# A new written order of all steps, and PSUM as four buffers whose halves serve single-bank steps

## The chip, the cores and the metric

The kernel runs on one core of a Trainium2 chip. The metric is the device time of one execution in microseconds (us). Five engines take part, each with its own instruction queue that is worked off in order: PE (TensorE, matrix products and transposes; the profile shows its weight loads apart, as PEld), ACT (ScalarE), DVE (VectorE), POOL (GpSimd) and SP (SyncE), which here only issues DMA transfers. An engine waits at an instruction until everything that the instruction needs is there, and what stands behind it in the same queue waits too.

## What is computed

Blockwise causal attention over 8 batches, 8 heads, 576 positions and 64 dimensions, followed by a gated unit with a causal convolution in its gate. Cut to what matters:

```python
scores = q @ k.transpose(0, 1, 3, 2) / sqrt(64)
scores = where(block_i >= block_j, scores, -1e9)      # blocks of 64 positions
attn = softmax(scores)
x = (attn @ v).transpose(0, 2, 1, 3).reshape(8, 576, 512)
gate_pre = sum(conv_w[k] * xp[:, k:k + 576, :] for k in range(5))   # xp: x with 4 zero rows ahead
gate = 1 / (1 + exp(-gate_pre))
out = (gate * (x @ w_val)) @ w_out
```

## The kernel before

The work is cut into steps. A step is a Python function under `@op` that issues a few instructions of one kind on one engine; the text `PLAN` lists all 961 steps in the order in which they are issued. A word such as `S/1.0/P/2` means: step `S`, for pair 1, part 0, on PE, into PSUM buffer 2. `V`, `A`, `G`, `S`, `P` stand for DVE, ACT, POOL, SP and PE. Each engine's queue is the list's words for that engine, in the list's order, so nothing is planned at run time: the list is the plan. The framework adds the waits between engines that the data and the buffers ask for.

Attention works on 32 pairs of heads (four pairs to a batch). For a pair `p`:

- `lq`, `lk`, `lv` load its q, k and v (256 KB, 256 KB and two of 128 KB). `lt` and `lvt` load the last 64 positions of all heads of a batch. All are issued by SP, but for one `lk` of ACT.
- `cq`, `cv`, `ct`, `cvt` cast what was loaded to fp16, mostly on POOL (`cq0` is pair 0's `cq` in two halves).
- `T` transposes q and k on PE (8 transposes of 128 columns) into one PSUM bank; `Te` copies the result to SBUF. `T0`, `T0e` are the same for pair 0 in halves; `TT`, `TTe` for the tails of a batch.
- `S/p.t` (t = 0, 1, 2) forms scores with 64 contraction rows, both heads side by side in two banks; `E/p.t` takes their exponential on ACT (128 x 1024 elements). `SL`, `EL` are the last key block of all heads of a batch. `mka`, `mkb` write zeros over the masked corners, on POOL.
- `A` (30 products of 65 columns) multiplies by v, with a column of ones that yields the sums; `N` divides on DVE; `X` transposes the result back on PE (5 transposes) and `Xe` copies it to the gated unit's input.

The gated unit works on 16 half batches `n`: `C` (80 products on 32 x 32 pieces of the array) is the convolution into two 2-bank buffers, `CS` the gate's tanh on ACT, `V` the value projection (8 products of 288 columns, two steps per `n`), `Ve` the product of both on DVE. `O` is the output projection of 128 rows (4 products of 512 columns), `Oe` copies it to SBUF, `Od` stores it; the last 128 rows go in two halves as `OL`, `OLe`, `OLd`. Once at the start, `CW` brings the convolution's weights onto partitions with a fp32 product, and `CWe` builds from them the pieces that `C` uses; `lwv`, `cwv` load and cast the value weights; `lwo`, `cwo`, `W`, `We` load, cast and reorder the output weights. `w0` is a filler: products of zeros that nothing reads. `pact` is an exponential of one element, ahead of which the activation table is loaded.

The loads and casts have few buffers: five for q and k, five for v, four for transposed q and k, four for exponentials, six for output rows, two for tails. SP's queue holds loads and stores together, so a store that waits for its copy holds the loads behind it.

PSUM has eight banks. Before, `PP` (line 142) makes three buffers of two banks, 0 to 2, and two of one bank, 3 and 4. A step that needs two banks (`S`, `SL`, `A`, `V`, half a `C`) takes a buffer of 0 to 2; a step that needs one bank (`T`, `X`, `TT`, `W`, `O`, `OL`) takes buffer 3 or 4, or the first bank of one of the others. `one(b)` (line 145) gives the bank of a single-bank step.

Single lines carry many steps: line 127 is every product, line 322 the transposes of `T`, 354 those of `TT`, 453 those of `X`, lines 192 and 194 every copy on ACT and on DVE or POOL, 388 `E`, 410 and 412 `mka`, 416 `mkb`, 444 and 445 `N`.

Of the kernel before, what the change touches and what calls it, by code (L numbers as in the profile page):

```python
# [12 lines left out]
lk/1/S pact//A ppool//G lq/1/S lk/0/A lq/0/S lt/0.1/S pdve//V cq0/1/A w0/14/P/4 cq/1/G lt/0.0/S  # L13
lk/2/S lcv//S lq/2/S T/1/P/2 cq/2/G Te/1/A lq/3/S cq0/0/V lk/3/S S/1.0/P/2 lvt/0/S T0/1/P/3 E/1.0/A
T0e/1/V S/1.1/P/1 T0/0/P/0 lk/4/S T0e/0/A E/1.1/A lt/1.0/S lt/1.1/S S/0.1/P/0 cq/3/V lq/4/S ct/0/G
E/0.1/A S/0.0/P/1 TT/0/P/2 lv/0.0/S TTe/0/V E/0.0/A T/2/P/3 lv/0.1/S lq/5/S S/0.2/P/0 SL/0/P/2
Te/2/V S/1.2/P/1 T/3/P/4 Te/3/V lk/5/S lv/1.1/S CW//P/3 lv/1.0/S cvt/0/G cv/0/V E/0.2/A lk/6/S
lq/6/S E/1.2/A S/2.1/P/0 lv/3.1/S mka/0/G S/2.2/P/1 lvt/1/S ct/1/G TT/1/P/4 lv/2.0/S lv/3.0/S EL/0/A
mkb/1/G E/2.1/A S/3.0/P/2 CWe//V cq/4/G mkb/0/G A/0/P/0 TTe/1/V E/2.2/A N/0/V S/3.1/P/1 T/4/P/4
cq/5/G S/2.0/P/0 mka/1/G cv/1/G E/3.0/A E/3.1/A T/5/P/3 mkb/2/G lv/2.1/S cq/6/G S/3.2/P/1 E/2.0/A  # L20
Te/4/V lv/4.1/S mka/3/G E/3.2/A Te/5/V A/1/P/2 SL/1/P/0 S/4.1/P/1 EL/1/A T/6/P/3 N/1/V mka/2/G
cv/2/V lk/7/S S/4.0/P/0 X/0/P/4 cvt/1/G lwo/1/S mkb/3/G cv/3/G lv/4.0/S Te/6/V E/4.1/A S/4.2/P/2
E/4.0/A mka/4/G A/2/P/1 A/3/P/0 lwo/0/S E/4.2/A S/5.1/P/2 cwo/1/G N/2/V X/2/P/3 lq/7/S S/5.0/P/1
lv/5.0/S cv/4/G lv/5.1/S mkb/4/G Xe/0/A lwv/0/S lwv/1/S N/3/V E/5.1/A cq/7/G Xe/2/V lv/6.0/S
S/5.2/P/0 lv/6.1/S cv/5/G E/5.0/A X/3/P/4 Xe/3/V E/5.2/A X/1/P/3 lq/8/S A/4/P/2 lk/8/S Xe/1/V lk/9/S
N/4/V mkb/5/G C/0/P/1+0 CS/0.1/A T/7/P/3 S/6.0/P/2 X/4/P/4 lq/9/S CS/0.0/A lt/2.0/S S/6.2/P/0
cwo/0/G Te/7/V lt/2.1/S Xe/4/V E/6.0/A cwv/1/V lv/7.1/S S/6.1/P/1 E/6.2/A mka/5/G lv/7.0/S W/1/P/3
cwv/0/G E/6.1/A mka/6/G A/5/P/2 mkb/6/G We/1/A V/0.0/P/0 cv/6/G N/5/V cq/8/G cq/9/G S/7.1/P/1
W/3/P/3 W/2/P/4 Ve/0.0/V E/7.1/A lvt/2/S S/7.2/P/0 A/6/P/2 lk/11/S E/7.2/A S/7.0/P/1 ct/2/G W/0/P/0
lv/8.1/S We/2/V cv/7/G We/3/V lq/11/S E/7.0/A T/8/P/3 X/5/P/4 mka/7/G N/6/V Te/8/A lt/3.1/S lv/8.0/S  # L30
lk/10/S C/1/P/1+2 We/0/V S/8.1/P/0 Xe/5/V mkb/7/G TT/2/P/4 CS/1.0/A cq/11/G X/6/P/3 lq/10/S CS/1.1/A
V/0.1/P/1 E/8.1/A TTe/2/V lt/3.0/S Ve/0.1/V S/8.0/P/2 lv/12.0/S T/9/P/4 Xe/6/V E/8.0/A A/7/P/0
mka/8/G S/8.2/P/2 lk/12/S SL/2/P/1 O/0.0/P/3 Te/9/V O/0.1/P/4 EL/2/A E/8.2/A lq/13/S N/7/V cvt/2/G
lv/10.0/S S/9.1/P/0 S/9.2/P/1 mkb/8/G Oe/0.1/V Oe/0.0/A X/7/P/3 E/9.1/A Xe/7/V lv/11.1/S V/1.0/P/2
lv/9.1/S cv/8/G lv/9.0/S E/9.2/A Ve/1.0/V A/8/P/0 ct/3/G S/9.0/P/1 E/9.0/A T/11/P/3 lv/10.1/S
cq/10/G lt/4.1/S Te/11/A mkb/9/G T/10/P/4 lt/4.0/S N/8/V C/2/P/0+2 Te/10/V V/1.1/P/1 CS/2.0/A
lq/12/S S/10.0/P/0 Ve/1.1/V lt/5.1/S CS/2.1/A cv/9/G lq/16/S S/10.1/P/2 E/10.0/A lk/13/S E/10.1/A
TT/3/P/4 mka/9/G TTe/3/V lk/14/S S/10.2/P/1 mka/10/G cv/10/G O/0.3/P/3 E/10.2/A mkb/10/G lv/11.0/S
A/9/P/0 S/11.0/P/2 Oe/0.3/V lk/16/S N/9/V E/11.0/A S/11.1/P/1 lv/14.0/S cq/12/G O/0.2/P/4 A/10/P/0
lq/14/S lk/17/S Oe/0.2/V lv/13.0/S cq/13/G S/11.2/P/2 lq/15/S cv/11/G lv/12.1/S N/10/V T/12/P/3  # L40
lvt/4/S X/8/P/4 E/11.1/A C/3/P/1+0 E/11.2/A mkb/11/G cq/14/G Xe/8/A mka/11/G SL/3/P/2 CS/3.0/A
lvt/3/S Te/12/V EL/3/A CS/3.1/A X/10/P/4 Od/0.1/S lt/5.0/S T/13/P/3 V/2.1/P/1 lv/13.1/S S/12.1/P/2
Xe/10/V Te/13/V V/2.0/P/0 Ve/2.1/V V/3.0/P/1 X/9/P/4 lk/15/S Ve/2.0/V Ve/3.0/V E/12.1/A lv/15.0/S
lv/16.1/S A/11/P/0 S/12.0/P/2 lk/18/S N/11/V S/12.2/P/1 E/12.0/A cv/12/G Od/0.0/S E/12.2/A ct/4/G
O/0.5/P/3 cvt/3/G V/3.1/P/0 Xe/9/V TT/4/P/4 lk/19/S Oe/0.5/V T/14/P/3 S/13.0/P/2 Ve/3.1/V mkb/12/G
TTe/4/A E/13.0/A S/13.1/P/1 lv/15.1/S X/11/P/0 Od/0.2/S Te/14/V mka/12/G lv/16.0/S E/13.1/A
O/0.4/P/4 A/12/P/2 cq/15/G Oe/0.4/A Xe/11/V N/12/V cv/13/G S/13.2/P/0 S/14.0/P/1 mka/13/G O/0.6/P/3
T/15/P/4 E/14.0/A C/4/P/1+2 Oe/0.6/V E/13.2/A mkb/13/G X/12/P/3 cq/16/G CS/4.1/A A/13/P/0 SL/4/P/2
# [12 lines left out]
Te/20/V E/18.0/A lk/25/S Od/0.6/S ct/6/G SL/5/P/0 EL/5/A S/19.0/P/1 cvt/5/G V/6.0/P/2 S/19.2/P/0
mka/18/G mkb/18/G E/19.0/A Ve/6.0/V X/17/P/4 E/19.2/A lq/25/S S/19.1/P/1 Xe/16/V A/18/P/2 cv/20/G
E/19.1/A T/21/P/3 N/18/V lv/22.1/S cv/19/G Te/21/A C/7/P/0+1 CS/7.1/A lq/27/S V/6.1/P/2 lt/7.1/S
T/22/P/3 mkb/19/G S/20.1/P/1 CS/7.0/A Xe/17/V S/20.0/P/0 Ve/6.1/V E/20.1/A E/20.0/A S/20.2/P/2
Te/22/V E/20.2/A O/1.3/P/4 Od/0.5/S V/7.0/P/1 O/1.2/P/3 mka/19/G mka/20/G Oe/1.3/A lk/24/S lq/26/S
S/21.0/P/0 lv/25.0/S cq/25/G cv/21/G E/21.0/A lv/24.0/S Ve/7.0/V Oe/1.2/V lv/24.1/S S/21.2/P/1
lq/24/S TT/6/P/4 mkb/20/G TTe/6/V E/21.2/A cq/23/G lt/7.0/S A/19/P/2 cq/24/G X/18/P/4 A/20/P/0
N/19/V lv/23.1/S N/20/V Xe/18/A lq/28/S lk/28/S Od/1.0/S S/21.1/P/1 S/22.1/P/2 E/21.1/A cv/22/G
lv/25.1/S Od/0.8/S X/19/P/3 O/1.4/P/4 E/22.1/A Xe/19/V Oe/1.4/V mka/21/G C/8/P/1+0 V/7.1/P/2 lq/30/S
CS/8.1/A Ve/7.1/V lv/27.0/S CS/8.0/A X/20/P/3 T/24/P/0 Te/24/V S/22.0/P/1 Xe/20/A SL/6/P/2 T/23/P/4  # L70
lv/27.1/S lk/26/S cv/24/G mkb/21/G O/1.5/P/3 lv/26.0/S cq/28/G S/22.2/P/0 Te/23/V E/22.0/A EL/6/A
A/21/P/1 E/22.2/A S/23.0/P/2 E/23.0/A V/8.0/P/0 T/25/P/4 lv/23.0/S Od/1.4/S N/21/V Ve/8.0/V Oe/1.5/V
# [32 lines left out]
def kernel(  # L105
# [11 lines left out]
    fp32 = mybir.dt.float32  # L117
# [27 lines left out]
    def one(b):  # L145
        return PP[b][0:128, 0]

# [461 lines left out]
```

## Time and profile before

| | |
|---|---|
| median of 3 runs | 201.42 us (200.97 to 202.28) |
| span of the profiled execution | 199.3 us |
| mean granted TensorE clock | 0.957 |
| read from and written to HBM | 30.42 MB and 9.44 MB |

The span runs from the first to the last instruction of one execution. The costliest groups of the profile, with busy time, mean length of one, and idle time ahead of them with its main releaser:

| group | count | busy us | mean ns | idle before us |
|---|---|---|---|---|
| ACT, exponential of scores (L388) | 96 | 93.7 | 1025 | 24.0, PE |
| PE, value projection (L127) | 256 | 37.3 | 291 | 0.0 |
| PE, output projection (L127) | 148 | 36.0 | 374 | 0.0 |
| PE, attention times v (L127) | 896 | 34.5 | 196 | 1.9, POOL |
| POOL, cast of q and k (L194) | 30 | 31.0 | 1043 | 15.4, DMA of q |
| DVE, copy of transposed q and k (L194) | 23 | 27.3 | 1196 | 4.1, PE |
| DVE, division (L445) | 32 | 26.4 | 824 | 1.1 |
| DVE, gate times value (L512) | 32 | 24.1 | 752 | 18.9, PE |
| PE, transposes of q and k (L322) | 256 | 20.8 | 228 | 2.6, POOL |
| DVE, copy of output rows (L194) | 28 | 19.1 | 688 | 10.4, PE |

A busy time of PE counts overlapping products whose ends are modelled; the distance from one product's start to the next says more. The slices of the profile cut the span into 40 equal parts of 5 us. The clock row gives what share of full speed PE was granted.

### The profile page before, as it was taken

What the parts mean: (1) busy time and instruction counts of PE and PEld (TensorE: products, weight loads), DVE (VectorE), ACT (ScalarE), POOL (GpSimd) and SP (SyncE); (2) the same over time, 40 slices, a digit from 0 to 9 for tenths busy, and PEclk for the clock granted to TensorE, in tenths of its full rate; (3) what the DMA queues carried; (4) which work ended last, traced back from release to release, by engine and by line L of the source; (5) the groups of instructions that cost most, each with busy time, mean ns of one, the idle gap of its engine ahead of it and who ended that gap; (6) DMA issues with size and microseconds to landing.
All of it is one profiled execution on the core that took longest, in us unless ns stands there. A gap on an engine that the chain in (4) does not pass through costs nothing.

```text
span 199.3 us, 8575 instructions
## 1 busy us (share of the span) xinstructions
PE 184.3 (92%) x3706; PEld 129.3 (65%) x3706; DVE 121.3 (61%) x193; ACT 139.4 (70%) x172; POOL 85.3 (43%) x201
## 2 busy tenths in 40 slices
PE   6389999699999799999999999999996999999992
PEld 3248677457676677767777776767764766676651
DVE  5047687675676676764666666777655383664562
ACT  3476896749779638798799888679694888643221
POOL 7255656763635535366394084282606041210000
PEclk9855899879999999999999999999999999999999
DMA  5999999999989999999969819991277610421445
GB/s 183 213 230 274 212 272 342 300 187 243 231 171 271 259 217 315 257 236 290 255 159 278 211 38 303 250 293 62 96 199 227 122 56 3 161 104 68 155 154 215
DMA packets 70336, 40.42 MB, mean 203 GB/s; under 512 B 48149, under 2 KB 64789, under 8 KB 70298
## 3 DMA queue, kind: packets, MB, share of 16 engines
q1 hardware_dynamic: 69882, 39.48, 77.6%
q8 instruction: 29, 0.48, 1.1%
q10 hardware_dynamic: 416, 0.39, 0.6%
q14 instruction: 9, 0.07, 0.1%
HBM read 30.42 MB, written 9.44 MB: 200 GB/s over the span
## 4 chain that ended last, share of the span: by engine, by line
PE 75%; DMA 9%; ACT 4%; POOL 4%; issue 3%; DVE 2%; SPq 1%; POOLq 0%; DVEq 0%; ACTq 0%
PE P L127 64%; PE P L322 7%; PE P L453 4%; DMA vs<-in_v_dram 3%; ACT pt L388 3%; DMA vts<-in_v_dram 3%; DMA qks<-in_q_dram 2%; PE P L354 1%; POOL qk L194 1%; DVE x L445 1%; ACT qkT L192 1%; POOL v16t L194 1%; POOL v L194 1%; POOL w_out L194 1%; POOL pt L410 0%
## 5 line engine op out<-in xcount | busy, mean ns | idle before, releaser
L388 ACT ACTIVATE pt<-P 128x1024 f16<-128x1024 f32 x96 | 93.7, 1025 | 24.0 <-PE P L127 22.9
L194 POOL CAST qk<-qks 128x1024 f16<-128x1024 f32 x30 | 31.0, 1043 | 15.4 <-DMA qks<-in_q_dram 10.9
L127 PE MATMUL P<-xt,w_val 128*128 128x288 f16 x256 | 37.3, 291 | 0.0
L127 PEld LDWEIGHTS <-pt 128*128 128x128 f16 x960 | 32.8, 99 | 5.9 <-issue 1.6
L127 PE MATMUL P<-v,pt 128*128 128x65 f16 x896 | 34.5, 196 | 1.9 <-POOL pt L410 0.9
L127 PE MATMUL P<-w_out,gv 128*128 128x512 f16 (+1 forms) x148 | 36.0, 374 | 0.0
L512 DVE SCALAR_TENSOR_TENSOR gv<-th,P 128x576 f16<-128x576 f32 x32 | 24.1, 752 | 18.9 <-PE P L127 15.0
L127 PE MATMUL P<-qkT 64*128 64x256 f16 (+3 forms) x256 | 31.8, 316 | 2.8 <-ACT qkT L192 1.8
L194 DVE COPY qkT<-P 128x1024 f16<-128x1024 f16 (+1 forms) x23 | 27.3, 1196 | 4.1 <-PE P L322 3.9
L127 PEld LDWEIGHTS <-w_val 128*128 128x128 f16 x256 | 23.8, 99 | 8.2 <-issue 1.1
L494 ACT ACTIVATE th<-P 128x576 f32<-128x576 f32 x32 | 19.2, 648 | 12.8 <-PE P L127 12.8
L127 PEld LDWEIGHTS <-qkT 64*128 64x128 f16 x512 | 17.0, 97 | 16.8 <-issue 10.0
L445 DVE TENSOR_TENSOR x<-P,rc 128x640 f16<-128x640 f32 x32 | 26.4, 824 | 1.1
L194 DVE COPY osb<-P 128x512 f32<-128x512 f32 x28 | 19.1, 688 | 10.4 <-PE P L127 8.3
L410 POOL MEMSET pt<- 64x256 f16 x32 | 9.8, 306 | 31.8 <-ACT pt L388 31.1
L322 PE MATMUL P<-ident,qk 128*128 128x128 f16 x256 | 20.8, 228 | 2.6 <-POOL qk L194 2.6
L444 DVE RECIPROCAL rc<-P 128x10 f32<-128x10 f32 x32 | 7.0, 220 | 25.0 <-PE P L127 23.7
L194 POOL CAST v<-vs 128x512 f16<-128x512 f32 x30 | 18.4, 619 | 8.3 <-DMA vs<-in_v_dram 5.0
L322 PEld LDWEIGHTS <-qk 128*128 128x128 f16 x256 | 16.1, 102 | 7.1 <-POOL qk L194 3.4
L127 PEld LDWEIGHTS <-gv 128*128 128x128 f16 x148 | 12.6, 98 | 12.2 <-issue 1.3
L127 PE MATMUL P<-xt,DG 32*32 32x288 f16 x1280 | 16.9, 288 | 0.0
L416 POOL MEMSET pt<- 64x128 f16 x32 | 6.5, 204 | 22.8 <-ACT pt L388 22.1
(57 smaller groups left out, 154.4 us busy)
## 6 DMA issues: line engine op xcount, KB each, us to landing
out_dram<-osb SPq DMA_DIRECT2D x35, 256.0 KB, 3.1
qks<-in_q_dram SPq DMA_DIRECT2D x32, 256.0 KB, 5.3
vs<-in_v_dram SPq DMA_DIRECT2D x64, 128.0 KB, 5.1
qks<-in_k_dram SPq DMA_DIRECT2D x31, 256.0 KB, 5.1
tls<-in_k_dram SPq DMA_DIRECT2D x8, 128.0 KB, 5.9
tls<-in_q_dram SPq DMA_DIRECT2D x8, 128.0 KB, 6.1
vts<-in_v_dram SPq DMA_DIRECT2D x8, 128.0 KB, 5.5
w_out_st<-in_moe_w_out_dram SPq DMA_DIRECT2D x2, 512.0 KB, 6.4
```

The source lines that it names most:

```text
L127: nc.tensor.matmul(out=out, lhsT=lhsT, rhs=rhs, start=start, stop=stop, skip_group_check=True)
L192: nc.scalar.copy(out=out, in_=in_)
L194: (nc.vector if eng == "V" else nc.gpsimd).tensor_copy(out=out, in_=in_)
L322: nc.tensor.transpose(out=r[:, o:o + 128], in_=t[0:128, c, 2 * i:2 * i + 2, 0:64], identity=ident16[0:128, 0:128])
L388: nc.scalar.activation(out=rot(pts, p)[0:128, 0:2, 512 * t:512 * t + 512], in_=PP[where.pop(("S", p, t))][0:128], func=AF.Exp, bias=0.0, s ...
L410: nc.gpsimd.memset(pt[64:128, 0:2, 0:1024].rearrange("p h (t s) -> p h t s", t=2)[:, :, :, 0:64], 0.0)
L416: nc.gpsimd.memset(rot(pts, p)[64:128, 0:2, 1024:1088], 0.0)
L444: nc.vector.reciprocal(out=rc[0:128], in_=r[:, :, :, 64:65])
L445: nc.vector.tensor_tensor(out=rot(x16, p)[0:128].rearrange("p i h d -> p h i d"), in0=r[:, :, :, 0:64], in1=rc[0:128].to_broadcast([128, 2 ...
L453: nc.tensor.transpose(out=half16(bank)[:, 128 * i:128 * i + 128], in_=rot(x16, p)[0:128, i, 0:2, 0:64], identity=ident16[0:128, 0:128])
L494: nc.scalar.activation(out=rot(ths, n)[0:128, 2 * i:2 * i + 2, 0:288], in_=PP[where["C", n][i]][0:128, 0:2, 0:288], func=AF.Tanh, bias=0.0 ...
L512: nc.vector.scalar_tensor_tensor(out=rot(gvs, b // 2)[0:128, 2 * y:2 * y + 2, b % 2, hf, 0:288], in0=rot(ths, n)[0:128, 2 * y:2 * y + 2, 0 ...
```

## The change

Three things change. The list `PLAN` is written anew: the same steps with the same work (each attention and gated-unit step occurs as often as before), in another order, some on another engine, and with other PSUM buffers. Seven filler words take the place of one. The copies of output rows (`Oe`) are 19 on ACT and 16 on DVE instead of 7 and 28; DVE casts q and k of pairs 1, 4 and 5 instead of pair 3, and does both `cwo`; POOL does both `cwv`; three of four `We` are on ACT. The first lines put `lcv` and `CW`, the convolution's weights, ahead of the loads and transposes of q and k, and `pact` behind the first transposes' copies.

PSUM becomes four buffers of two banks. Two-bank steps name a buffer 0 to 3; single-bank steps name a bank 0 to 7, which is half of a buffer. The filler `w0` takes its number of contraction rows as a second argument.

The diff, cut to what the text speaks of:

```diff
@@ PLAN
-lk/1/S pact//A ppool//G lq/1/S lk/0/A lq/0/S lt/0.1/S pdve//V cq0/1/A w0/14/P/4 cq/1/G lt/0.0/S
-lk/2/S lcv//S lq/2/S T/1/P/2 cq/2/G Te/1/A lq/3/S cq0/0/V lk/3/S S/1.0/P/2 lvt/0/S T0/1/P/3 E/1.0/A
-T0e/1/V S/1.1/P/1 T0/0/P/0 lk/4/S T0e/0/A E/1.1/A lt/1.0/S lt/1.1/S S/0.1/P/0 cq/3/V lq/4/S ct/0/G
-E/0.1/A S/0.0/P/1 TT/0/P/2 lv/0.0/S TTe/0/V E/0.0/A T/2/P/3 lv/0.1/S lq/5/S S/0.2/P/0 SL/0/P/2
-Te/2/V S/1.2/P/1 T/3/P/4 Te/3/V lk/5/S lv/1.1/S CW//P/3 lv/1.0/S cvt/0/G cv/0/V E/0.2/A lk/6/S
...
-cwo/0/G Te/7/V lt/2.1/S Xe/4/V E/6.0/A cwv/1/V lv/7.1/S S/6.1/P/1 E/6.2/A mka/5/G lv/7.0/S W/1/P/3
-cwv/0/G E/6.1/A mka/6/G A/5/P/2 mkb/6/G We/1/A V/0.0/P/0 cv/6/G N/5/V cq/8/G cq/9/G S/7.1/P/1
-W/3/P/3 W/2/P/4 Ve/0.0/V E/7.1/A lvt/2/S S/7.2/P/0 A/6/P/2 lk/11/S E/7.2/A S/7.0/P/1 ct/2/G W/0/P/0
...
-Od/1.2/S S/26.1/P/1 S/26.0/P/0 cq/29/G V/10.0/P/2 Xe/24/V lvt/7/S T/29/P/3 Te/27/A mka/25/G
-O/2.0/P/4 E/26.0/A lv/31.1/S S/26.2/P/0 Ve/10.0/V S/27.0/P/2 mkb/25/G cvt/7/G E/26.1/A A/25/P/1
-Oe/2.0/V Te/29/A E/26.2/A O/1.8/P/3 mka/26/G N/25/V S/27.2/P/0 cv/27/G E/27.0/A mkb/26/G A/26/P/2
...
-Oe/3.7/V OLe/1/A Od/3.4/S O/3.5/P/3 OLd/1/A O/3.6/P/4 Oe/3.5/V Od/3.7/S Oe/3.6/A OL/0/P/2 OLe/0/V
-Od/3.5/S Od/3.6/S OLd/0/S
+ppool//G lcv//S pdve//V CW//P/4 lk/0/S lk/1/S cq0/1/V lq/1/A cq/1/V T/1/P/6 Te/1/A lq/0/S lk/3/S
+cq0/0/V T0/0/P/5 T0/1/P/7 T0e/1/A lq/3/S cq/3/G lt/0.0/S w0/2.128/P/0 w0/2.128/P/0 S/1.1/P/0 T0e/0/V
+S/0.0/P/3 S/0.1/P/1 pact//A E/1.1/A lt/0.1/S ct/0/G E/0.0/A w0/2.64/P/5 T/3/P/0 lk/2/S TT/0/P/1
+lq/2/S lk/4/S TTe/0/V cq/2/G S/1.0/P/3 E/0.1/A mka/0/G E/1.0/A mka/1/G lq/5/S lk/5/S S/0.2/P/1
+SL/0/P/3 E/0.2/A Te/3/V S/3.2/P/0 T/2/P/5 E/3.2/A lq/4/S S/3.0/P/1 E/3.0/A w0/2.64/P/0 S/3.1/P/0
+lk/6/S lq/6/S S/1.2/P/1 EL/0/A lv/0.0/S cq/6/G mkb/0/G E/3.1/A cq/5/V T/5/P/6 E/1.2/A Te/2/V
+S/2.2/P/0 E/2.2/A CWe//V cq/4/V T/4/P/7 Te/5/V S/2.0/P/2 S/2.1/P/1 lv/0.1/S cv/0/V T/6/P/6 lvt/0/S
+cvt/0/G A/0/P/0 E/2.1/A Te/4/V S/4.0/P/1 E/2.0/A lt/1.0/S mkb/2/G lt/1.1/S ct/1/G N/0/V TT/1/P/4
+TTe/1/V X/0/P/7 Xe/0/V E/4.0/A mka/3/G mkb/1/G Te/6/A S/4.2/P/2 SL/1/P/1 EL/1/A S/4.1/P/0 E/4.1/A
+lv/1.1/S lq/7/S lv/1.0/S cv/1/G A/1/P/3 S/5.1/P/1 N/1/V lv/2.0/S mka/2/G lv/2.1/S cv/2/G A/2/P/0
+lk/7/S cq/7/G mkb/3/G E/4.2/A E/5.1/A S/5.2/P/3 S/6.1/P/2 E/6.1/A N/2/V S/5.0/P/1 T/7/P/0 Te/7/V
...
+Xe/2/V Xe/1/V X/3/P/6 Xe/3/V A/5/P/0 N/5/V mka/4/G S/6.2/P/1 mkb/4/G lv/4.1/S lv/4.0/S cv/4/G
+A/4/P/3 N/4/V E/6.2/A S/7.1/P/0 E/7.1/A lwv/1/S lq/8/S C/0/P/2+1 cwv/0/G cwv/1/G V/0.1/P/3 CS/0.1/A
+Ve/0.1/V C/1/P/1+0 X/5/P/6 CS/0.0/A lv/6.0/S cv/6/G mkb/6/G CS/1.1/A mka/6/G A/6/P/2 Xe/5/A lk/8/S
+cq/8/G T/8/P/0 lwo/0/S cwo/0/V X/4/P/1 V/1.1/P/3 lwo/1/S cwo/1/V CS/1.0/A Xe/4/A W/1/P/1 We/1/A
+W/0/P/2 We/0/A W/2/P/3 Te/8/V S/8.0/P/0 E/8.0/A N/6/V S/8.1/P/2 E/8.1/A lk/10/S lt/2.0/S lq/10/S
+W/3/P/2 Ve/1.1/V X/6/P/6 cq/10/G T/10/P/7 lt/2.1/S lk/9/S Te/10/A ct/2/G We/3/V lq/9/S cq/9/G
+V/0.0/P/0 TT/2/P/2 TTe/2/A Ve/0.0/V V/1.0/P/2 T/9/P/7 lv/7.1/S lq/13/S lk/12/S Xe/6/V S/10.1/P/0
+mka/7/G lv/7.0/S cv/7/G We/2/A E/10.1/A S/8.2/P/1 E/8.2/A Ve/1.0/V O/0.2/P/4 Te/9/V S/9.0/P/3
+E/9.0/A S/9.2/P/0 E/9.2/A lk/11/S lk/13/S lv/11.0/S lq/12/S O/0.0/P/5 Oe/0.0/A mkb/7/G mka/8/G
...
+Oe/2.0/A Od/1.6/S lv/31.0/S Xe/22/V T/29/P/2 Te/29/A V/9.1/P/2 C/10/P/0+3 CS/10.0/A mkb/24/G
+CS/10.1/A A/24/P/1 Ve/9.1/V lk/31/S Od/2.0/S Od/1.5/S S/26.2/P/0 E/26.2/A N/24/V S/26.0/P/2 E/26.0/A
+TT/7/P/6 O/2.2/P/7 C/11/P/1+0 TTe/7/V SL/7/P/2 EL/7/A lq/31/S lvt/7/S mkb/25/G mkb/26/G lv/31.1/S
+O/1.7/P/6 T/28/P/4 cvt/7/G CS/11.1/A CS/11.0/A Oe/2.2/V Oe/1.7/V Od/1.7/S X/24/P/5 Te/28/A lv/30.1/S
+lv/29.1/S mka/25/G mkb/27/G A/25/P/0 S/27.0/P/3 E/27.0/A N/25/V S/29.0/P/1 lv/27.1/S cv/27/G
+mka/26/G O/2.1/P/4 Oe/2.1/V V/10.0/P/0 Ve/10.0/V E/29.0/A S/29.2/P/1 cq/31/G S/28.1/P/3 Xe/24/A
...
+O/3.3/P/0 Oe/3.3/A Od/3.3/S V/14.1/P/1 O/3.7/P/1 Ve/14.1/V Oe/3.7/A Od/3.7/S OL/1/P/0 OLe/1/V
+O/3.5/P/5 Oe/3.5/A OLd/1/A Od/3.5/S O/3.6/P/4 Oe/3.6/A Od/3.6/S O/3.4/P/2 Oe/3.4/A Od/3.4/S OL/0/P/3
+OLe/0/A OLd/0/S w0/14.128/P/2 w0/2.128/P/1 w0/2.128/P/6
@@ PSUM
-    PP = [psum.tile([128, 2 if i < 3 else 1, 512], fp32, tag=f"P{i}", name=f"P{i}")
-          for i in range(5)]
+    PP = [psum.tile([128, 2, 512], fp32, tag=f"P{i}", name=f"P{i}") for i in range(4)]
 
     def one(b):
-        return PP[b][0:128, 0]
+        return PP[b // 2][0:128, b % 2]
@@ fillers
-    def w0(n, eng, bank):
+    def w0(n, k, eng, bank):
         for _ in range(n):
-            mm(one(bank)[:, 0:256], wz[0:128, 0:128], wz[0:128, 0:256])
+            mm(one(bank)[:, 0:256], wz[0:k, 0:128], wz[0:k, 0:256])
```

## The prediction

> **What bounds the kernel now.** I read the page's shares and slices first, then five-microsecond windows, then the timeline at every place where PE stops.
>
> ```profile
> PE 184.3 (92%) x3706; PEld 129.3 (65%) x3706; DVE 121.3 (61%) x193; ACT 139.4 (70%) x172; POOL 85.3 (43%) x201
> ...
> PE   6389999699999799999999999999996999999992
> ...
> PEclk9855899879999999999999999999999999999999
> ```
>
> PE is the bound: above 90% in nearly every slice, the others far below. What can be won lies in the slices with a low PE digit or a low clock digit. The windows (columns after the length: PE, PEld, DVE, ACT, POOL busy with counts, clock, DMA share, GB/s):
>
> ```profile
> 10.00:15.00 5.00, 4.01 (x40) 2.47 (x38) 2.12 (x4) 3.75 (x5) 2.56 (x5) 0.50 1.22 228
> 15.00:20.00 5.00, 5.00 (x58) 4.11 (x52) 3.58 (x5) 3.34 (x4) 2.52 (x6) 0.50 1.19 276
> ...
> 35.00:40.00 5.00, 3.40 (x57) 2.32 (x56) 2.92 (x3) 3.85 (x5) 3.98 (x10) 0.87 1.16 296
> 40.00:45.00 5.00, 4.89 (x70) 2.85 (x69) 3.80 (x7) 2.35 (x3) 3.04 (x4) 0.78 1.11 189
> ```
>
> From 10 to 20 us PE is busy but at half clock, and ACT idles a third of the time; around 37 us PE stops and the clock falls again. The timeline names the stops (start, length, what, idle before it and its releaser):
>
> ```profile
> 20.49 0.95 PE L127 MATMUL P<-v,pt 128*128 128x65 f16 x14
> ...
> 38.06 0.39 PE L127 MATMUL P<-w_out,idfold 32*32 32x512 f16 x3 [1.49 <-issue]
> ```
>
> ```profile
> 68.06 0.29 PE L127 MATMUL P<-kt 64*128 64x64 f16 x8 [1.14 <-ACT th L494]
> ```
>
> ```profile
> 149.31 0.62 POOL L194 CAST v16t<-vts 128x512 f16<-128x512 f32 x1 [6.44 <-DMA vts<-in_v_dram]
> ...
> 150.35 0.32 PE L127 MATMUL P<-v,pt 128*128 128x65 f16 x5 [0.92 <-POOL pt L410]
> ```
>
> The first row is A/0, the first attention product. The last two: POOL waited 6.4 us for lvt/7, which SP issued only at 143.42, behind output stores; the masks of A/26 queue behind that cast.
>
> **A ruler for PE.** PE's starts, laid on the written order, give each step's length at full clock where nothing waits: A 0.915, V and C 0.98, O 0.865, T 0.447, X 0.28, TT 0.225, S 0.217/0.220/0.230, SL 0.126, OL 0.437, W 0.21, CW 0.9. A step followed by one with another number of contraction rows takes 0.095 more (V then X 0.98, V then S 1.075; O then A 0.865, O then S 0.96); leaving a 32-row step costs nothing more. All steps without fillers: 156.6 us. Before has 146 paid changes (13.9), so 170.5. The last projection ends at 195.4; 24.9 us are lost on the way, 3.8 follow it (last copy, store, end): 199.2. Lost so far: 14.0 at A/0 (20.49 less 6.5 of work), 15.9 at C/0, 20.0 at C/1 (45.66 less 25.6: the W stop and 3.4 us of half clock cost 4.1), 1.3 more at 68, 1.9 at 150, 1.6 in crumbs.
>
> **The change, part by part.**
>
> *Fewer changes of row count.* The new order has 125 paid changes: 21 x 0.095 = 2.0 us off, work 168.5.
>
> *The start.* The 14 fillers at 1.2 us go; CW (fp32, 1.9 us at half clock) takes their idle time: it needs only the 10 KB load, now SP's first, and ident16. Cost nothing, hidden by the wait for q and k; the third 256 KB load lands at 5.76 as before, and CW's cover would have to run 2 us over to matter. cq/1 moves to DVE (0.69 against POOL's 1.04): T/1 at about 6.5, at half clock (0.97), Te/1 (1.01) to 8.7. T0/0, T0/1 and four 256-column fillers (0.21 each at half clock) end at 9.65. `pact` now stands behind T0e/1 on ACT: the table load (1.28) and its activation (0.20), formerly hidden in the first 2 us, hold every Exp queued behind them until 11.05; the first Exp was at 9.38.
>
> From there ACT's queue sets the pace: until E/6.2, which frees the buffer of C/0, it has 23 E at 0.96, two EL at 0.60, one Te at 1.02: 24.4 us, so C/0 at 35.5 at best. ACT will not be fed without a gap: from S/1.1 to A/0 PE has 6.5 us of work, nearly all T and S. Before, such a stretch (13.10 to 20.49) took 7.39 us for 4.16 of ruler, 1.78 times. That is 11.6 us from 9.65; with its waits for E I walk A/0 to 23.6 and E/4.0 to 26.1, 1.9 late. C/0 at 37.4 (bounds 35.5, and 39 if the half clock lasts until 28). Loads do not set it: summed in SP's new order at the old landing spacing, lwv/1 lands near 34, cwv ends by 35.3. Work done at C/0 is 19.7: lost 17.7, against 20.0 before once W was past.
>
> On the clock the Trainium skill speaks twice, in "TensorE: Matmul & The Clock Gate". Part 1 says one busy window of about 3.4 us releases full speed; Part 4 says transposes do not count as busy the same way. Here PE was busy through 15 to 20 us at 0.50, so the first alone is not borne out; the second agrees, since release came at 21.7, 1.2 us after A/0. By the first the start would be the second rival.
>
> *W.* W no longer shares one-bank buffers with T; its casts move to DVE (cwo), We mostly to ACT. lwo/1 lands near 39.3, the cast ends by 40, W/1 is due at 43.4: no stop. But ACT then has three We, seven E, Te, TTe and Oe between W/1 and X/7: 1.8 + 6.7 + 1.0 + 0.6 + 0.6 = 10.7, with hand-over 11.0, against 10.25 of PE work: 0.8 lost.
>
> *PSUM halves.* T, X, TT, W, O may now sit in any of eight banks, S, V, A, C in four pairs. It adds no instruction. A pair step must find both halves read. Where I compare each PE-ACT/DVE-PE path with the PE work between its ends, the short ones sum to 2.4 us; the same sum before is 2.5, where the trace shows 1.6 of crumbs. I take 2.0 (0 to 4).
>
> *Engines.* Twelve Oe move from DVE (0.69) to ACT (0.60). ACT's whole sum rises by 6 us to 145 of some 195: no bound later on, but nearly full from 11 to 60 us.
>
> *Late loads.* SP still issues lvt/7 and lv/27.1 behind Od/1.6 and Od/1.7. From Oe/1.6: issues 0.55 each, landing 5.4, cvt 0.62, mka 0.46, against the PE work to A/25: 1.7 late; lv/27.1 blocks A/26 by 2.0 in the same way. The first wait pays most of the second: 2.0 together (bounds 0, and 3.7). Nothing for the unexplained stop at 68 (0 to 1.3): 0.6.
>
> *The end.* OLe/0 moves to ACT behind Oe/3.4: 0.3 later. The 18 fillers after OL/0 (0.107 each, 1.9 us) start once Oe/3.4 has read their bank and run beside the last store (2.0 after its issue): nothing; without that cover at most 1 us.
>
> Sum: 168.5 + 17.7 + 0.8 + 2.0 + 2.0 + 0.6 + 4.1 = 195.7 against 199.2. The median stood 2.2 above the span (201.4): 197.9, 1.8% faster.
>
> **Rivals.**
>
> *Slower: the clock stays at half until C/0.* PE will be ACT's follower from 24 to 37 us, with gaps, and S, T and X between the A. From A/0 to C/0 there are 11.6 us of work; at 1.78 that is 20.6, C/0 at 44.2: 6.8 later, 204.7. It decides from C/0 at 41 on: there the gain is gone. For: before lost its clock at 38.75 after one thin window. Against: A's share of the work there is as in 26 to 33 us before, which kept full clock. 0.12.
>
> *Faster: the fillers win the clock early.* Four full-row matmuls at 9 us might do for release what A/0 did; then ACT runs unbroken, C/0 at 35.5, and with few crumbs 195.0. 0.15.
>
> *Same: ACT's full stretch breaks.* From C/0 to T/11 the loads reach their casts within 0.5 to 1.5 us of need, and ACT is full; one late cast passes to all behind it. At two such waits of 1.5 us each: 200.9. 0.18.
>
> *It does not do what it says:* the halves are guarded by whole buffers. Then 52 neighbouring one-bank steps would wait for the other half's copy, 40 us in sum, say half of it on the path: near 218. No row before has a step in one half while the other is being read. The Trainium skill ("PSUM — Partial Sum Buffer", the rule under bank collisions) asks for guards by bank, which speaks against it; no run here shows it. 0.03.
>
> **How the numbers follow.** My forecast has 0.52, its own range 195.5 to 200.5. The range leaves out the whole-buffer case, the upper part of the slower one and the lowest tenth: 194.5 to 203.5. One per cent is about what a measurement of this kernel tells from no change: faster below 199.4, slower above 203.4. Faster: nine tenths of the forecast and the early clock, 0.62. Same: the broken stretch, the forecast's rest and the slower case's mild end, 0.22. Slower 0.16.
>
> **What would show it.** First Exp near 11 us behind the table load; ACT above 90% from 12 to 37; A/0 near 23.6, C/0 near 37.4; clock 0.50 until 25 to 28 and 1.00 after, with no fall at W; POOL waiting some 2 us for vts or vs before A/25 or A/26; the last projection ending near 191.6. I am wrong if C/0 comes after 41, if PE stops for more than 7 us in all behind it, or if X and T wait for the other half of their buffer.

## The result, and the profile after

The changed kernel takes 234.69 us (median of 4 runs, 232.0 to 237.1) where the kernel before took 201.19 beside it. Two of the four, the profiled one among them, were slow runs (235.8 and 237.1), so the ratio is taken over the other two (232.0 and 233.5): 1.158 times as long, 95% interval 1.146 to 1.170. The profiled execution spans 234.1 us. These are the rows of its page that answer to those shown of before:

```profile
PE 191.7 (82%) x3718; PEld 133.8 (57%) x3718; DVE 117.3 (50%) x185; ACT 144.8 (62%) x182; POOL 83.7 (36%) x199
...
PE   3677788668879887899898799837879888999976
...
PEclk9999999976979997999999999995899999999999
```

The work is what it was; PE's share fell from 92% to 82%. The slices show it to the very end: 7s and 8s in place of a nearly unbroken row of 9s, and four dips of the clock where before had one behind the start. No engine has become the bound: ACT has 5 us more to do, but is busy for only 62% of the span.

The start came as forecast: A/0 at 22.47 us (forecast 23.6), C/0 at 37.32 (37.4). At T/10, 51.78, 24.4 us had been lost by the ruler of the prediction. At the last projection, 230.00, it was 61.9. So the time went behind the start and all along it, some 2 us for every 10 on average, though not evenly (10 us between 150 and 171 us, 8 between 50 and 70, 1 to 4 in the other stretches of 20 us). What PE waits for there is seen in the groups of instructions (the last column is the idle time ahead of the group, with what ended most of it):

```profile
L128 PE MATMUL P<-w_out,gv 128*128 128x512 f16 (+1 forms) x148 | 38.8, 390 | 5.7 <-ACT osb L192 2.1 <-DVE qkT L194 1.2 <-ACT qkT L192 1.1
...
L322 PE MATMUL P<-ident,qk 128*128 128x128 f16 x256 | 22.1, 236 | 11.3 <-issue 2.6 <-DVE xt L194 2.5 <-DVE qk L194 2.5
...
L453 PE MATMUL P<-ident,x 128*128 128x128 f16 x160 | 14.2, 222 | 5.0 <-DVE qkT L194 1.3 <-DVE x L445 1.0 <-DVE osb L194 0.8
```

The first row is the output projection. It reads `gv` and `w_out` and writes a bank. It would need the copy of transposed q and k (`qkT`), which ended 2.3 us of its waits, only if it took over the bank that is being copied, and here it doesn't: O/0.5 writes bank 1 while T/16 lies in bank 0, and O/1.5 writes bank 1 while T/26 lies in bank 0. Before, this group waited 0.0 us in all, and the third (X, which here waits for `qkT` and for output rows `osb`) 0.1:

```profile
L127 PE MATMUL P<-w_out,gv 128*128 128x512 f16 (+1 forms) x148 | 36.0, 374 | 0.0
...
L453 PE MATMUL P<-ident,x 128*128 128x128 f16 x160 | 13.8, 220 | 0.1
```

The timeline names the steps. Here are the last projections (start, length, engine, what, idle before it and its releaser):

```profile
224.62 0.59 ACT L192 COPY osb<-P 128x512 f32<-128x512 f32 x1 [1.26 <-PE P L128]
225.26 1.46 PE L128 MATMUL P<-w_out,gv 128*128 128x256 f16 x8 [0.67 <-ACT osb L192]
...
227.44 1.89 PE L128 MATMUL P<-w_out,gv 128*128 128x512 f16 x8 [0.72 <-ACT osb L192]
...
230.00 0.60 PE L128 MATMUL P<-w_out,gv 128*128 128x256 f16 x4 [0.67 <-ACT osb L192]
```

The ACT row is Oe/3.7, which reads bank 1. PE starts OL/1 0.05 us after its end, and OL/1 writes bank 0, the other half of the same buffer. O/3.6 (bank 4) waits in the same way for Oe/3.5 (bank 5), OL/0 (3) for Oe/3.4 (2). The first such wait stands in the first ten microseconds, T0/1 (bank 7) behind Te/1 (bank 6):

```profile
8.29 1.01 ACT L192 COPY qkT<-P 128x1024 f16<-128x1024 f16 x1 [5.80 <-PE P L322]
...
9.35 0.59 PE L322 MATMUL P<-ident,qk 128*128 128x128 f16 x4 [0.67 <-ACT qkT L192]
```

The semaphores of the built program agree: T0/1 waits for ACT's first copy, and 66 waits in all are for an access to the other half of the same buffer, 27 of them PE's, the rest the copies'. The list decides which way round: when the other half's copy stands ahead of a step, the step waits for the copy; when it stands behind, the copy waits for the step.

I then put each wait of PE over 0.2 us (a step's distance beyond the ruler) down to what its semaphores say came last. After: 17.3 us end on the other half, 22.5 on a dependency of the step's own bank or data, 7.1 on a stop in which no semaphore was unmet (below), 9.0 on nothing named, much of it steps run at half clock; 55.9 together. ("After" is the changed kernel.)

### The profile page after: what moved, and what is told of

It reads as the page before. It is cut to its first block, busy times and chain, and to the rows that moved or that the text cites. A ratio compares the mean times of both kernels' runs of the same rounds, so it can differ in the third digit from the quotient of the medians.

```text
span 234.1 us, 8561 instructions
## 1 busy us (share of the span) xinstructions
PE 191.7 (82%) x3718; PEld 133.8 (57%) x3718; DVE 117.3 (50%) x185; ACT 144.8 (62%) x182; POOL 83.7 (36%) x199
## 4 chain that ended last, share of the span: by engine, by line
PE 49%; ACT 14%; DVE 11%; DMA 10%; issue 8%; POOL 4%; SPq 3%; POOLq 0%; DVEq 0%; ACTq 0%
PE P L128 41%; ACT pt L388 9%; DMA qks<-in_k_dram 5%; DVE qkT L194 5%; PE P L322 5%; DMA qks<-in_q_dram 3%; PE P L453 3%; ACT osb L192 2%; DVE x L445 2%; DMA tls<-in_q_dram 2%; POOL qk L194 2%; DVE xt L194 1%; DVE osb L194 1%; ACT xt L192 1%; SPq L207 1%
## 5 line engine op out<-in xcount | busy, mean ns | idle before, releaser
L128 PE MATMUL P<-w_out,gv 128*128 128x512 f16 (+1 forms) x148 | 38.8, 390 | 5.7 <-ACT osb L192 2.1
L194 DVE COPY qkT<-P 128x1024 f16<-128x1024 f16 (+1 forms) x24 | 28.8, 1200 | 23.8 <-PE P L322 12.7
L128 PE MATMUL P<-xt,w_val 128*128 128x288 f16 x256 | 38.3, 298 | 0.4 <-ACT pt L388 0.2
L194 POOL CAST qk<-qks 128x1024 f16<-128x1024 f32 x28 | 29.4, 1060 | 20.8 <-DMA qks<-in_q_dram 13.6
L128 PE MATMUL P<-qkT 64*128 64x384 f16 (+3 forms) x256 | 31.3, 310 | 6.2 <-ACT pt L388 2.3
L322 PE MATMUL P<-ident,qk 128*128 128x128 f16 x256 | 22.1, 236 | 11.3 <-issue 2.6
L128 PEld LDWEIGHTS <-w_val 128*128 128x128 f16 x256 | 25.0, 102 | 9.9 <-issue 1.4
L322 PEld LDWEIGHTS <-qk 128*128 128x128 f16 x256 | 17.9, 106 | 12.5 <-issue 8.5
L192 ACT COPY osb<-P 128x512 f32<-128x512 f32 x19 | 11.2, 590 | 19.8 <-PE P L128 11.3
L192 ACT COPY qkT<-P 128x1024 f16<-128x1024 f16 (+1 forms) x9 | 8.7, 965 | 16.5 <-PE P L322 15.9
L128 PE MATMUL P<-xt,DG 32*32 32x288 f16 x1280 | 17.3, 296 | 1.8 <-issue 1.0
L410 POOL MEMSET pt<- 64x256 f16 x32 | 10.2, 320 | 22.9 <-ACT pt L388 22.0
```

The lines of the kernel that those rows point to most:

```text
L128: nc.tensor.matmul(out=out, lhsT=lhsT, rhs=rhs, start=start, stop=stop, skip_group_check=True)
L192: nc.scalar.copy(out=out, in_=in_)
L194: (nc.vector if eng == "V" else nc.gpsimd).tensor_copy(out=out, in_=in_)
L322: nc.tensor.transpose(out=r[:, o:o + 128], in_=t[0:128, c, 2 * i:2 * i + 2, 0:64], identity=ident16[0:128, 0:128])
L410: nc.gpsimd.memset(pt[64:128, 0:2, 0:1024].rearrange("p h (t s) -> p h t s", t=2)[:, :, :, 0:64], 0.0)
```

## The experiments

Theory: the halves of a buffer are not independent; the program's waits guard a tile of PSUM as a whole. Rivals: the new order itself (other waits, a fuller ACT, late loads), or the clock. Times are medians, beside the kernel before on the same chip; where neither an interval nor a number of runs is given, of one run.

**One tile.** One edit: the declaration of PSUM. Built like this, the program has no wait left for the other half, and keeps those within a bank.

```diff
-    PP = [psum.tile([128, 2, 512], fp32, tag=f"P{i}", name=f"P{i}") for i in range(4)]
+    PB = psum.tile([128, 8, 512], fp32, tag="P", name="P")
+    PP = [PB[0:128, 2 * i:2 * i + 2] for i in range(4)]
```

> Edit: the changed kernel with its order, engines and banks untouched; only the declaration of PSUM differs: one tile of eight banks, of which the four buffers are slices, in place of four tiles of two banks. In the built program every wait of one half's step for the other half of its buffer then goes (66 of them stand in the changed kernel, counted from its semaphores), and the waits between accesses of one bank stay. Theory (the halves are not independent: TensorE's single-bank steps, and the copies, wait for the other half's copy): the 31.7 us of TensorE waits over 0.25 us in the profile of after that no dependency by bank explains go, and with them most of the 20.5 us at half clock: 196 to 205 us. Rival 1 (the order itself: the other waits, ACT at 145 us of the 234, the late loads): above 225. Rival 2 (the clock falls because of what the order does to TensorE, not because of the waits): 215 to 225, with the four stretches at half clock still in the record.

Measured: 202.8 us (201.0 to 205.2), 1.009 of before (1.004 to 1.014). Its page and its groups of instructions:

```profile
PE 183.7 (91%) x3718; PEld 130.8 (65%) x3718; DVE 115.7 (57%) x185; ACT 143.6 (71%) x182; POOL 83.6 (42%) x199
...
PE   3787899629999999998999999997999999999996
...
PEclk9998899976999999999999999999999999999999
```

```profile
L128 PE MATMUL P<-w_out,gv 128*128 128x512 f16 (+1 forms) x148 | 36.2, 374 | 0.0
...
L323 PE MATMUL P<-ident,qk 128*128 128x128 f16 x256 | 21.9, 236 | 3.7 <-DVE qk L195 2.3 <-issue 1.1 <-DVE x L446 0.2
...
L454 PE MATMUL P<-ident,x 128*128 128x128 f16 x160 | 14.2, 223 | 0.6 <-DVE x L446 0.6
```

The same instructions in the same order and banks, and some 30 us are gone (1.158 of before against 1.009): the projections wait for nothing, X for its own data. By the account above PE's waits are 23.3 us now: 0 for other halves, 9.7 true ones, 7.7 stops, 5.9 unnamed. The fall of 32.6 matches that of the two profiles' spans (234.1 to 201.4). About half of it, 17.3, were direct waits; 12.8 were true waits that had grown. They grew by the waits for the other half, the only thing that differs; that it went by way of the copies, which hold 39 of the 66 waits, is likely but no run takes those out alone. The 20.5 us at half clock all lay behind 49 us, and behind 50 us none is left: these dips followed the waits. (Two dips earlier on, 10.2 us together, are new.) My figure of 31.7 us in the expectation was put together wrongly, though: it held the 7 us of stops, which stayed, and left out the grown waits.

**Larger tiles.** The same order with two tiles of four banks.

```diff
+    PB = [psum.tile([128, 4, 512], fp32, tag=f"P{i}", name=f"P{i}") for i in range(2)]
+    PP = [PB[i // 2][0:128, 2 * (i % 2):2 * (i % 2) + 2] for i in range(4)]
```

> Edit: the changed kernel with PSUM declared as two tiles of four banks, two buffers in each; order, engines and banks untouched. In the built program the waits for another bank of the same tile grow from 66 to 325. Theory (steps wait for whatever else lies in their tile): a larger tile means more such waits, on the two-bank steps too: at least 20 us above the changed kernel, 255 to 330. Rival (the loss lies in the order, and the tile is of no matter): within 3 us of the changed kernel's 234.7.

Measured: 398.98 us, above my range. The page's PE row, and the scores' row of its groups of instructions:

```profile
PE 250.4 (63%) x3718; PEld 167.4 (42%) x3718; DVE 116.7 (29%) x185; ACT 149.4 (38%) x182; POOL 82.4 (21%) x199
```

```profile
L128 PE MATMUL P<-qkT 64*128 64x384 f16 (+3 forms) x256 | 41.1, 373 | 50.4 <-ACT pt L389 20.8 <-DVE qkT L195 12.3 <-DVE x L446 6.5
```

The scores now wait 50.4 us (1.4 in the first run), in good part for steps on banks of their tile that they don't use; the rest are waits of their own that have grown. The mean granted clock fell to 0.807, which lengthens the run further. With 0, 66 and 325 such waits the same order takes 203, 235 and 399 us. It is the tile that is guarded, not a pair of banks. That the tile of eight banks is guarded by bank is what its semaphores show; why it is treated otherwise the runs don't tell.

**The kernel before, with pairs.** Its order, but the single buffers 3 and 4 as halves of one tile.

```diff
+    PP = [psum.tile([128, 2, 512], fp32, tag=f"P{i}", name=f"P{i}") for i in range(4)]
     def one(b):
-        return PP[b][0:128, 0]
+        return PP[b][0:128, 0] if b < 3 else PP[3][0:128, b - 3]
```

> Edit: the kernel before, its order and start untouched, with the changed kernel's PSUM: buffers 3 and 4, which were two tiles of one bank, become the two halves of a fourth tile of two banks. Nothing else. Theory: the 99 waits for the other half that this adds to the built program (about 45 of them TensorE's) cost this order too, though less than the changed order's 66, since here only two of eight banks are paired with single-bank steps on both sides, and its list was laid out for single banks: 205 to 235. Rival (four buffers of two banks cost nothing by themselves and the order is to blame): within 1% of 201.2.

Measured: 222.9 us, 1.109 of before (1.102 to 1.115). From its groups of instructions:

```profile
L127 PE MATMUL P<-w_out,gv 128*128 128x512 f16 (+1 forms) x148 | 36.4, 373 | 8.5 <-DVE qkT L193 3.6 <-ACT xt L191 2.0 <-DVE osb L193 1.3
...
L452 PE MATMUL P<-ident,x 128*128 128x128 f16 x160 | 13.9, 219 | 3.5 <-DVE qkT L193 1.3 <-DVE xt L193 0.8 <-ACT osb L191 0.8
```

The projection waits for `qkT` here too: 21 us for two paired banks, with nothing of the new order.

**Control: the kernel before in one tile.**

```diff
+    PB = psum.tile([128, 8, 512], fp32, tag="P", name="P")
+    PP = [PB[0:128, 2 * i:2 * i + 2] for i in range(4)]
```

> Edit: the kernel before with its eight banks declared as one tile of eight, cut into the same three double and two single buffers. Control for the first run: the waits in the built program are the same as the kernel before's, one for one. Theory: one tile by itself neither costs nor gains: within 1% of 201.2. Rival (a tile of eight banks changes something else, say how TensorE's writes are placed or signalled): more than 1% off, and the first run would then have two causes.

Measured: 202.2 us, 1.005 of before (1.001 to 1.010). One tile by itself gains nothing; so the 30 us of the first run come from the waits.

**What is left.** The first run should have given the forecast's 197.9 and is 5 us above it. Its timeline of PE around C/0 has the place:

```profile
35.16 0.71 PE L128 MATMUL P<-xt,DG 32*32 32x288 f16 x45
37.55 0.62 PE L128 MATMUL P<-xt,DG 32*32 32x288 f16 x35 [1.68 <-issue]
38.09 1.15 PE L128 MATMUL P<-xt,w_val 128*128 128x288 f16 x8
39.18 1.05 PE L128 MATMUL P<-xt,DG 32*32 32x288 f16 x80
40.17 0.44 PE L454 MATMUL P<-ident,x 128*128 128x128 f16 x5
44.29 0.93 PE L128 MATMUL P<-v,pt 128*128 128x65 f16 x14 [3.68 <-POOL qk L195]
```

PE stops in the middle of C/0, where no instruction waits for a semaphore, and again for 3.8 us ahead of A/6. The releaser named there, a cast of q and k, is not one that A/6 waits for: its masks were ready at 36.96 and its buffer at 39.4. What the two have in common is their distance: 128 products with 128 weight loads, 256 instructions of PE's stream. And packets of the instruction queue (16 KB each) landed at 36.02 and 42.87, 1.5 and 1.4 us before PE went on.

> Edit: the first run's kernel with 32 more dummy matmuls of 8 columns behind CW, in TensorE's first idle time, so that every later instruction stands 64 places further in TensorE's stream. Theory (the stops are at block limits of the instruction stream): they move back by 32 matmuls in the program, from C/0's 45th matmul to its 13th and from A/6's first to about C/1's 53rd, and still stand 256 instructions apart. Rival (they belong to the steps or to a wait): they stay at C/0's 45th matmul and at A/6. The time is of no matter here (200 to 206).

```diff
+    def wt(n, eng, bank):
+        for _ in range(n):
+            mm(one(bank)[:, 0:8], wz[0:128, 0:128], wz[0:128, 0:8])
...
+CW//P/4 wt/32/P/0 ...
```

The timeline of PE:

```profile
34.34 0.33 PE L128 MATMUL P<-xt,DG 32*32 32x288 f16 x13
35.56 0.93 PE L128 MATMUL P<-xt,DG 32*32 32x288 f16 x67 [0.89 <-issue]
...
37.51 0.78 PE L128 MATMUL P<-xt,DG 32*32 32x288 f16 x53
41.21 0.45 PE L128 MATMUL P<-xt,DG 32*32 32x288 f16 x27 [2.93 <-issue]
```

The run took 199.8 us. The stops moved to the 13th product of C/0 and the 53rd of C/1, to the product as expected. They belong to the instruction stream. The same limit is found in the kernel before: its stops at 38.06 and 68.06, which the prediction quoted, stand five blocks apart to the instruction.

Next, the loads, which I held to be what delays the packets. This kernel leaves out the loads of the two weight matrices and computes the gated part with zeros:

> Edit: the first run's kernel without the four loads of w_val and w_out (512 KB each); the two casts read a tile of zeros instead, so the gated part is computed with zero weights. All other instructions stay. In the first run TensorE stops for 2.0 us inside C/0 (to 37.55) and for 3.9 us ahead of A/6 (to 44.29) with no semaphore unmet; both stops end 1.4 to 1.5 us after a 16 KB packet of the instruction queue has landed, and stand 256 TensorE instructions apart. Theory (TensorE waits for its next block of instructions, whose packet waits its turn among the loads, which at this place take up to 8.3 us from issue to landing): with 2 MB less to load the packet comes sooner, the two stops together shrink from 5.9 us to below 3, and the time to 195 to 200. Rival (the stops belong to the steps, C's 80 small matmuls say): they stay at 5 us or more.

Measured: 200.1 us. From the timeline of PE:

```profile
36.64 0.44 PE L455 MATMUL P<-ident,x 128*128 128x128 f16 x5
40.21 0.85 PE L128 MATMUL P<-v,pt 128*128 128x65 f16 x14 [3.13 <-POOL pt L414]
```

The stop in C/0 shrank to 0.3 us, the one ahead of A/6 stayed at 3.35: neither theory as put. From entering a block until the next could run took 6.2 us, against 6.0 and 6.7 in the first run. But the DMA engines had not become idle, since the later loads had only moved up. So the next kernel leaves those out too, and computes with what its buffers hold:

```diff
-lk/9/S ... lk/31/S lq/9/S ... lq/31/S lv/9.0/S ... lv/31.1/S lt/2.0/S ... lt/7.1/S lvt/2/S ... lvt/7/S
```

> Edit: the kernel of e6_no_weight_loads without the loads of q, k and v of pairs 9 to 31 and of the last rows of batch entries 2 to 7 as well; the later pairs are computed from what the buffers still hold. All instructions of the five engines' own work stay, and the DMA engines should be nearly idle from about 33 us until the first output rows. In e6_no_weight_loads TensorE took 6.2 us from entering one block of 256 instructions to running the next ahead of A/6, and stopped for 3.35 us. Theory (the packet waits its turn among the loads): the turn ahead of A/6 falls to 4.5 us or less and the stop below 1.7. Rival (the turn takes its time whatever the DMA engines carry): the turn stays at 5.5 us or more and the stop at 2.5 or more.

Measured: 192.9 us. The windows from 35 to 40 us, first of the kernel without weight loads, then of this one (columns after the length: PE, PEld, DVE, ACT, POOL busy with counts, clock, DMA share, GB/s), and this one's timeline of PE:

```profile
35.00:40.00 5.00, 2.08 (x91) 1.43 (x90) 2.89 (x3) 2.60 (x5) 4.88 (x7) 1.00 0.88 212
```

```profile
35.00:40.00 5.00, 4.46 (x162) 3.57 (x144) 3.37 (x5) 3.22 (x6) 4.88 (x8) 1.00 0.04 8
```

```profile
37.26 0.44 PE L444 MATMUL P<-ident,x 128*128 128x128 f16 x5
38.25 0.58 PE L117 MATMUL P<-v,pt 128*128 128x65 f16 x14 [0.54 <-POOL qk L185]
```

With the DMA share at 0.04 the turn takes 3.6 us: the packet starts 1.0 us after the block is entered (4.1 in the first run), lands 1.15 later, and PE goes on after another 1.45. The stop is 0.8 us. So the packet does wait among the loads, and even on idle DMA engines a block must last some 3.6 us, going by this one stop, if PE is not to stop. C is 160 instructions in 1 us: the block with C/0's end, V/0.1 and C/1 is used up in 2.9. That gave the next kernel, in which C/1 comes later:

```diff
-C/0/P/2+1 ... V/0.1/P/3 ... C/1/P/1+0 X/5/P/6 ... A/6/P/2 ... T/8/P/0 ... X/4/P/1 V/1.1/P/3 ... W/1/P/1
+C/0/P/2+1 ... V/0.1/P/3 ... X/5/P/0 ... A/6/P/2 ... T/8/P/2 ... X/4/P/1 ... V/0.0/P/3 ... W/1/P/3 ... C/1/P/2+1
```

> Edit: the kernel of e9_shift32 (changed order, one tile of eight banks, 32 small dummy matmuls in TensorE's first idle time) with C/1, the second of the two steps of 80 small matmuls, moved from behind V/0.1 to behind A/6, T/8, X/4, V/0.0, three W and S/8.0, and the buffers of these steps reassigned so that no bank is written before it is read. Theory (a block of 256 TensorE instructions must last longer than its successor takes to arrive, 5 to 7 us here): the block that lasted 3.0 us now has 4.7 us of work, so the stop of 3.2 us ahead of it falls below 1.7 and the time is 1 to 2.5 us below e9_shift32's: 197 to 200. Rival (the loads of this stretch set the pace in any case, so time saved at the stop is lost waiting for lwo, lk/10 and lk/9): within 0.5 us of the same kernel without the move.

> The kernel of e9_shift32 again, timed: its one look gave 199.8, 3 us below the first run's median and 2 below the kernel before's. Theory (the 32 small matmuls fill TensorE's idle time before the first transposes, so the clock that was full from 11.6 us stays so until 42.3 without the window at half that the first run had at 18.5): 199 to 201, 0.5 to 1% below the kernel before. Rival (the one look was a fortunate run; kernels here spread by 2%): 201.5 to 203.5, as the first run.

Measured: 198.6 us for the one with C/1 moved (197.2 to 202.4), 0.984 of before (0.976 to 0.992); 200.7 for the one without, 0.998 (0.992 to 1.003). The timeline of PE with C/1 moved:

```profile
39.30 0.78 PE L128 MATMUL P<-xt,w_val 128*128 128x288 f16 x5
41.28 0.53 PE L128 MATMUL P<-xt,w_val 128*128 128x288 f16 x3 [1.21 <-issue]
...
43.56 0.61 PE L128 MATMUL P<-qkT 64*128 64x512 f16 x2 [1.40 <-DVE gv L518]
```

The block lasts 4.5 us and the stop behind it 1.5; without the move its stop was 3.2 in one profile and 4.5 in the other. By the medians on that chip the version with C/1 moved is 2.1 us below the one without, as expected, and 1.6% below the kernel before, though single times overlap. The one without has the time expected of it but is no faster than the kernel before beside it, and the window at half clock, whose absence was to explain that time, is back in its profile (18.2 to 21.6 us). The wait of 1.4 us at 43.56 with C/1 moved (S/8.0 for Ve/0.0) I tried to take out too, by moving S/8.0, W/3 and X/6:

> Edit: the kernel of e10_spread with S/8.0 moved from ahead of C/1 to behind it and W/3, X/6 ahead of V/1.1, banks reassigned to suit; in e10_spread S/8.0 waited 1.4 us for the copy Ve/0.0 of the buffer that it takes over, with C/1 queued behind it. Theory (that wait is on the path): it goes, and the time falls by 0.5 to 1.5 us, to 197 to 198.5. Rival (TensorE's next block of instructions or ACT's queue of CS, We and E takes its place): within 0.5 us of 198.6.

The wait is gone from its profile, whose span is 194.9 us, but the six times spread from 196.7 to 203.1 with a median of 201.2 beside 202.1 for the kernel before: undecided, and with it whether the gain of the version above holds on another chip.

**The fillers at the start.** The first run's kernel without its four early filler words (two products each, eight in all; the twelve of the expectation is a slip):

```diff
-w0/2.128/P/0 w0/2.128/P/0 S/1.1/P/0 ... w0/2.64/P/5 T/3/P/0 ... w0/2.64/P/0 S/3.1/P/0
+S/1.1/P/0 ... T/3/P/0 ... S/3.1/P/0
```

> Edit: the first run's kernel (changed order, one tile of eight banks) without the four filler words ahead of the first A (12 dummy matmuls between 8 and 16 us); the fillers at the end stay. Theory (the second rival's mechanism: full-row matmuls at 9 us win the clock early; the first run's clock record shows full speed from 11.7 us, the kernel before's from 21.7): without them the record shows half clock past 15 us, and C/0, which came at 35.2, comes 1 to 3 us later; 203.5 to 206 against the first run's 202.8. Rival (CW and T at the start and the loads set the clock and C/0, fillers do nothing): C/0 within 0.5 us of 35.2 and the time within 1% of 202.8.

Measured: 204.0 us, 1.003 of before (0.996 to 1.009), against 1.009 with the fillers: no difference. The windows, first without, then with fillers:

```profile
10.00:15.00 5.00, 3.44 (x50) 2.45 (x50) 2.15 (x3) 4.37 (x5) 2.81 (x7) 0.76 1.10 342
15.00:20.00 5.00, 4.31 (x46) 3.00 (x46) 4.86 (x7) 4.52 (x6) 2.35 (x3) 0.50 1.31 185
```

```profile
10.00:15.00 5.00, 4.27 (x60) 2.73 (x57) 2.41 (x4) 5.00 (x6) 3.11 (x6) 1.00 1.10 343
15.00:20.00 5.00, 3.58 (x48) 2.58 (x47) 4.97 (x7) 4.48 (x6) 2.33 (x4) 0.85 1.24 199
```

In these two profiles half of the theory holds: without fillers the clock record shows 0.50 from 12.6 to 22.9 us, with them from 18.5 to 21.9. But C/0 comes at 35.78 instead of 35.16. ACT is busy for 8.9 us of these ten without fillers and 9.5 with them, so it is likely that ACT sets the pace there and a faster PE only waits for it. One profile's clock is not the order's, though: the kernel before goes to full speed at 21.7 us in its profile, its control in one tile, with the same order, at 15.4.

## Why the prediction was wrong, point by point

**The step that failed** is the one on PSUM's halves. "A pair step must find both halves read", it said, and put 2.0 us (0 to 4) on it: I costed the banks' own paths and took it that one half's step need not heed the other. It must, in this program: the changed kernel loses some 30 us by it (1.158 of before against 1.009). Two of the signs that the prediction named came true: X and T wait for the other half, and PE stops far longer than 7 us behind C/0. The last rival described just this, with 52 steps, 40 us in sum and half of it on the path, and got 0.03. Its price of some 20 us was near the direct waits, 17.3, and short of the whole since I let only PE's steps wait: true waits grew by another 12.8 us, probably because the copies wait for the other half's steps too.

The Trainium skill ("PSUM — Partial Sum Buffer", "PSUM bank collisions raise a hardware error") says that PSUM is to be guarded by bank. I let that speak against the rival. The one-tile run is guarded in this way, and takes 202.8; but a page on what the chip needs says nothing of what the program's waits guard. I had written that no row of before has a step in one half while the other is read. An untried condition that meets some 50 steps wanted a wide price, not 0 to 4.

**The start**: first Exp at 11.37 us, forecast 11.05, but for another reason. The table load ran at 1.2 us and held nothing; T0/1's wait for the other half held the chain. Without that wait the first Exp comes at 9.72 and C/0 at 35.16. So C/0 at 37.4 came true in the changed kernel by luck, by two errors that cancelled. ACT was not above 90% up to there either (76% from 20 to 25 us).

**The early clock** (the second rival) was right: full speed from 12.15 us, half until 25 to 28 had been forecast. Its result was not: the fillers' run shows no time won by it. Nor did the reading hold by which the prediction tied the release in before to A/0, with transposes not counting: in the control in one tile, the same order, release comes at 15.4 us, 3.5 ahead of A/0 at 18.88.

**W**: 0.8 us lost, said the forecast. In the first run 8.7 us go from C/0 to T/10, 5.8 in the two stops of the instruction stream and more at the half clock that follows. I had seen the stop of before here and put it down to W, and left the one at 68 "unexplained".

**Crumbs, late loads and the unexplained stop**, 4.6 us together: 4.9 in the first run, by luck, since they lie elsewhere than I put them (0.6 us at A/25, nothing at A/26, a stop of 1.3 of the instruction stream at 137.26). **The tail**: 4.1, measured 3.9.

Set against the first run's span, the terms give 195.7 - 2.2 (C/0) + 7.9 (W) + 0.3 - 0.2 = 201.5, and it is 201.4. The order was costed within 6 us, the start too dear and W too cheap; the waits that come with the buffers were not seen.

## What to carry to other kernels

When buffers are split, merged or shared, look in the built program's semaphores for who waits for whom before any work on the order: the language may guard a tile as one, and here the same instructions took 203, 235 or 399 us by the tile's size alone. In a profile the mark is a group that waits for a tensor that it doesn't read and whose bank it doesn't take over. And steps of many short instructions were better spread here than put side by side.

## What the runs showed of the hardware

PE's instructions come in blocks of 256, one 16 KB packet each. In the profiles read here, PE stopped where it used up a block before the next had come: 3.6 us after entering it with the DMA engines idle (one stop), 4 to 7 us among the loads. It went on 1.3 to 1.6 us after the packet had landed. The profile calls such a stop "issue" or names an engine that happened to end nearby. The Trainium skill ("Runtime: NRT & Kernel Launch", "Instruction fetch mechanics") has the blocks of 256 and calls the cost of crossing one mostly hidden. In the first run 25 of 29 limits cost less than 0.3 us; the two around the steps C cost 5.8 together, and one of them 4.5 in another run.
